# Reordering the first batch's loads and copying block rows of four heads by one DMA, in a block-sparse attention and gated MLP kernel

## The chip, the cores and the metric

The kernel runs on one core of a Trainium2 chip. The core has a matrix engine (TensorE, in the profile PE, with its weight loads as PEld), VectorE (DVE), ScalarE (ACT), GpSimd (POOL) and SyncE (SP), which here only issues DMAs. Sixteen DMA engines move data between device memory and the on-chip memory SBUF. The metric is the device time of one execution in microseconds (us); the time of a kernel is the median of its runs.

## What is computed

The reference is a block-sparse attention (BigBird) followed by a spatial gating MLP (gMLP), cut here to what matters:

```python
# q, k, v: (B=4, H=8, S=768, D=64); blocks of 32 positions, 24 of them
scores = q @ k.T / sqrt(D)
mask = |blk_i - blk_j| <= 1 or blk_i in (0, 23) or blk_j in (0, 23)
mask |= blk_j in sampled_blocks[blk_i]           # 3 drawn blocks per query block
attn = softmax(where(mask, scores, -1e9))
x = (attn @ v) with heads side by side           # (4, 768, 512)

h = relu(x @ w_in)                               # (4, 768, 1024)
u, v = h[..., :512], h[..., 512:]
v_n = (v - mean(v)) / sqrt(var(v) + 1e-6)
v_s = w_spatial @ v_n + b_spatial[:, None]       # over the positions
out = (u * v_s) @ w_out                          # (4, 768, 512)
```

## The kernel before

**Heads and pairs.** The 32 heads of the four batches are taken in 16 pairs p; pairs 0 to 3 are the first batch. For each pair k, q and v are loaded as float32 (tiles `st_k`, `st_q`, `st_v`, made in `load`, L104 to L108), cast to bfloat16 by GpSimd (`cast`, L116 to L135; k and q into a tile `nat`, v into one of six tiles `vv`), and k and q are transposed so that the head dimension lies on the partitions. A load of one pair's k, q or v is 384 KB. Positions are taken in six chunks of 128 (`NCH` = 6), and queries of the first batch in three thirds of two chunks (`NT` = 3, `TC` = 2, `TW` = 256). `C01` are the chunks of the first third, `C03` the first four chunks, `C45` the last two.

**The mask as extra rows of the product.** The tile `kq` has 88 partitions: 64 rows of the transposed k and q and 24 rows (`MR`, one for each block) that carry the mask. Its free dimension is 8 heads times 1536 columns: 768 of k (`K_`) and 768 of q. In the k columns the 24 rows tell the block of each key; in the q columns they hold 0 for an allowed and -300 for a forbidden block. A product over 88 rows gives masked scores at once. These rows are the same for each head. They are made for head 0 (k part by VectorE at L199, the query part by TensorE and a copy, third by third: `mask_rows`, L296; the first two thirds, at L322 and L326, are copied by ScalarE, the last in slot 7) and copied from head 0 to the others by `rows` (L237 to L242), on VectorE in this kernel. `ROWS` (L690) lists those copies as (slot, first head, end head, columns). Pairs of later batches write only the 64 rows of k and q and reuse the mask rows.

**Slots.** The attention runs in slots, one exponential on ScalarE in each. In the first batch, slots 0 to 35, one slot makes scores of 128 x 1024 (`qk_unit`, L389 to L410: four products into one of two PSUM buffers, then the exponential at L410) for a unit of three slots: units 0 and 1 are the heads 0 and 1 with two thirds of the queries, then come pairs 1 to 3 with their first third (slots 6 to 14), pairs 1 to 3 with the second, and all pairs with the last third. The products with v (`av_unit`, L451) follow some four slots behind. From slot 36 on a slot is one chunk of keys of a head (`qk_full`, L418 and L422, and `av_full`, L469). Between them lie the MLP's products (L543), dealt out over the slots from a queue.

**What the change touches.** The order is written out by hand: each engine executes its instructions in the order of the program, and waits for what it needs. `when(slot, ...)` (L684) hangs further work on a slot: `tr_first(p)` (L347) transposes k and the first query third of pair p and copies them into `kq` by VectorE (slots 3, 6, 9 for pairs 1, 2, 3); `tr_rest(p)` (L355) does the other thirds (slots 11, 14, 16, and 17 for pair 0's last); the MLP's first steps, which need the weights `w_in_t`, start in slot 15. The loads of the first batch and of W_in are issued ahead of all slots: at L138 to L149 and, between the casts, at L252 to L275. All but two go by SyncE's queue, and the casts that they feed stand in the same stretch in GpSimd's order.

Of the kernel before, what the change touches and what calls it, by code (L numbers as in the profile page):

```python
# [10 lines left out]
FP32 = mybir.dt.float32  # L11
# [15 lines left out]
def kernel(  # L27
# [16 lines left out]
    nc = tc.nc  # L44

    B, H, S, D = q.shape
    BLK = 32
    NB = S // BLK
    NR = sampled_blocks.shape[1]
    NCH = S // 128  # L50
# [4 lines left out]
    NDM = DM // 128  # L55
# [8 lines left out]
    TC = NCH // NT  # L64
    TW = TC * 128
# [5 lines left out]
    work = ctx.enter_context(tc.tile_pool(name="work", bufs=1))  # L71
# [8 lines left out]
    b_col = const.tile([128, NCH], FP32)  # L80
    mhalf = const.tile([128, NCH], FP32)

    kq = const.tile([KR, H, 2 * S], BF16, name="kq")
    NVV = 6
    vv = [const.tile([128, 2, NCH, VS], BF16, name=f"vv{s}") for s in range(NVV)]
    MR = slice(D, KR)
    K_, Q_ = slice(0, S), slice(S, 2 * S)

    def qcols(t0, n=1):
        return slice(S + t0 * TW, S + (t0 + n) * TW)  # L90


    st = {}

    def dram(src, p, hs=slice(0, 2), cs=slice(0, NCH)):
        b, g = divmod(p, NG)
        return src[b, 2 * g + hs.start:2 * g + hs.stop].rearrange(
            "h (p c) d -> p h (c d)", c=NCH)[:, :, cs.start * D:cs.stop * D]

    H0, H1, BOTH = slice(0, 1), slice(1, 2), slice(0, 2)  # L100
    ALLC, C01, C03, C45 = slice(0, NCH), slice(0, TC), slice(0, 2 * TC), slice(2 * TC, NCH)
    SRC = {"k": k, "q": q, "v": v}

    def load(p, nm, hs=BOTH, cs=ALLC, eng=nc.sync):  # L104
        if (nm, p) not in st:
            st[nm, p] = work.tile([128, 2, S // 2], FP32, tag="st_" + nm, bufs=3, name="st_" + nm)
        eng.dma_start(out=st[nm, p][:, hs, cs.start * D:cs.stop * D],
                      in_=dram(SRC[nm], p, hs, cs))  # L108

# [3 lines left out]
    def nat0_view():  # L113
        return nat[0].rearrange("p c h d -> p (c h d)").rearrange("p (h x) -> p h x", h=2)

    def cast(p, nm, eng, hs=BOTH, cs=ALLC):  # L116
        if nm == "v":
            dst = vv[p % NVV][:, hs, cs, 0:D]
        else:
            if p not in nat:  # L120
                nat[p] = work.tile([128, 2 * NCH, 2, D], BF16, tag="nat", bufs=4, name="nat")
            c0 = 0 if nm == "k" else NCH
            dst = nat[p][:, c0 + cs.start:c0 + cs.stop].rearrange("p c h d -> p h c d")[:, hs]
        src = st[nm, p].rearrange("p h (c d) -> p h c d", d=D)[:, hs, cs]
        if p == 0 and nm != "v":
            dst = nat0_view()[:, hs, (c0 + cs.start) * D:(c0 + cs.stop) * D]
            if cs is not C45:
                dst = dst[:, 0].rearrange("p (i t d) -> p t i d", t=2, d=D)
                src = src[:, 0].rearrange("p (t i) d -> p t i d", t=2)
            else:  # L130
                dst = dst.rearrange("p h (c d) -> p h c d", d=D)
        if eng is nc.scalar:
            nc.scalar.activation(out=dst, in_=src, func=AF.Copy)
        else:
            eng.tensor_copy(out=dst, in_=src)  # L135

    samp = const.tile([KR, 2 * NR], I32)
    load(0, "k", H0, C03, eng=nc.scalar)  # L138
    load(0, "q", H0, C03, eng=nc.scalar)
    nc.sync.dma_start(out=samp[MR], in_=_listify(sampled_blocks).bitcast(I32))  # L140
    load(0, "k", H0, C45)
    load(0, "k", H1)
    load(0, "q", H1, C03)
    load(1, "k")
    load(1, "q")
    load(0, "v")
    load(2, "k")
    load(2, "q")
    load(1, "v")  # L149


    eq = const.tile([KR, NR + 1, NB], FP32)
# [56 lines left out]
    PL, DV = nc.gpsimd, nc.vector  # L209
# [10 lines left out]
    def w_load(key, src):  # L220
        wst[key] = work.tile([128, DM], FP32, tag="osb", bufs=6, name="w_f")
        nc.sync.dma_start(out=wst[key], in_=src)

    def w_in_load(u, g):
        w_load((u, g), moe_w_in[g * 128:(g + 1) * 128, 0 if u else DH:DH if u else DFF])

    def w_in_cast(u, g, eng):
        eng.tensor_copy(out=w_in_t[:, g, 0 if u else DH:DH if u else DFF], in_=wst.pop((u, g)))
# [8 lines left out]
    def rows(hs, cs, eng=nc.vector):  # L237
        src = kq[MR, 0:1, cs].to_broadcast([NB, hs.stop - hs.start, cs.stop - cs.start])
        if eng is nc.scalar:
            nc.scalar.activation(out=kq[MR, hs, cs], in_=src, func=AF.Copy)  # L240
        else:
            eng.tensor_copy(out=kq[MR, hs, cs], in_=src)  # L242
# [7 lines left out]
        nc.gpsimd.memset(vv[s][:, :, :, D:VA], 1.0)  # L250
    nc.gpsimd.memset(mhalf, -0.5)
    cast(1, "k", PL)  # L252
    cast(1, "q", PL)
    cast(0, "v", PL)
    load(3, "k")
    cast(2, "k", PL)
    cast(2, "q", PL)
    cast(1, "v", PL)
    load(3, "q")
    cast(3, "k", PL)  # L260
    cast(3, "q", PL)
    load(2, "v")
    load(0, "q", cs=C45)
    load(3, "v")
    cast(2, "v", PL)
    cast(3, "v", PL)
    cast(0, "q", PL, cs=C45)
    pieces = [(u, g) for u in range(2) for g in range(NDM)]
    for i, x in enumerate(pieces):
        if i >= 6:  # L270
            w_in_cast(*pieces[i - 6], PL)
        w_in_load(*x)
    for x in pieces[2:]:
        w_in_cast(*x, PL)
    nc.sync.dma_start(out=b_col, in_=moe_b_spatial.rearrange("(p c) -> p c", c=NCH))  # L275

# [8 lines left out]
    def bank(nm="ps", tag=None):  # L287
        return psum.tile([128, 1024], BF16, tag=tag or moe_tag(), bufs=2 if tag else 1, name=nm)
# [13 lines left out]
    def head(ps, h, c0, n, at=0):  # L302
        for i in range(0, n, 2):
            nc.tensor.transpose(out=ps[:, at + i * 64:at + (i + 2) * 64],
                                in_=nat0_view()[:, h, (c0 + i) * D:(c0 + i + 2) * D],
                                identity=ident)

    def split0(ps, h, c0, n, t, copy=dve_copy):
        w = n * 64
        copy(kq[0:D, h, c0 * 128 + t * w:c0 * 128 + (t + 1) * w], ps[t * D:(t + 1) * D, 0:w])  # L310
# [14 lines left out]
    split0(psq, 0, *Q4, 1)  # L325
    m1()  # L326

    def second():
        ps2 = bank("ps2", "av")
        head(ps2, 0, *K2)  # L330
        for t in range(2):
            split0(ps2, 0, *K2, t)
        rows(H1, K_)
        rows(H1, qcols(0, 2))
# [349 lines left out]
    def when(slot, *fns):  # L684
        at.setdefault(slot, []).extend(fns)

    def c(f, *a, **kw):
        return lambda: f(*a, **kw)

    ROWS = [(2, 3, 4, K_), (2, 2, 4, qcols(0)), (2, 4, 8, K_), (4, 4, 8, qcols(0, 2)), (13, 2, 4, qcols(1, 2)), (17, 4, 8, qcols(2)),  # L690
            (20, 1, 2, qcols(2))]
    when(0, second)
    when(1, third)
    when(1, c(rows, slice(2, 3), K_))
    when(2, lambda: filler(FILL3, psum.tile([128, 512], FP32, tag=moe_tag(), bufs=1, name="wps")))
    for p, sl in ((1, 3), (2, 6), (3, 9)):
        when(sl, c(tr_first, p))
    for sl, h0, h1, cs in ROWS:
        when(sl, c(rows, slice(h0, h1), cs))
# [64 lines left out]
    def slot_of(p):  # L764
        return S0 + 12 * (p - NG)

    for p in range(NG, NP):
        g = slot_of(p)
# [76 lines left out]
```

## Time and profile before

| what | value |
|---|---|
| runs | 213.68, 212.82, 215.3 us, median 213.68 |
| profiled execution | 212.75 us, its span 210.6 us |
| granted TensorE clock | 0.996 of full speed |
| DMA | 41.82 MB, mean 199 GB/s; 62868 of 63323 packets on the queue of SyncE |
| loads (L107), 384 KB | 4.6 (k), 5.2 (q), 5.7 (v) us median from issue to landing |
| transposes by DMA | 6.7 us (`tt`), 2.8 us (`xt`), 3.1 us (`gt`) median to landing |

The span is what the profile shows of the execution; the metric is about 2 us longer. A row of an order of time reads: start in us, duration in us, engine, line, operation, output<-inputs with partitions x elements, and how many instructions are merged; in brackets the idle time of the engine before it and what ended it. A row of the chain of waits reads: start, duration, engine, output, line. A row of waits reads: who waited, for whom, us in total, times, longest.

### The profile page before, as it was taken

The page shows a single profiled execution, that of the slowest core. Times are in us where ns is not written, and L with a number is a line of the kernel's source. Part 1 is how long each engine was busy: PE and PEld are TensorE (multiplying, and loading weights), DVE is VectorE, ACT ScalarE, POOL GpSimd, SP SyncE. Part 2 cuts the span into 40 slices and gives each one's busy share as a digit, 9 for nine tenths or more (in the row PEclk, how much of TensorE's full clock was granted, in tenths as well). Part 3 has the DMA queues.
Part 4 walks back from the last instruction along what each step waited for, and adds up shares of the span by engine and source line. Part 5 has one row for each costly group of instructions (what it writes and reads, how often), then busy time and mean ns, then how long its engine had stood idle before and what let it go on. Part 6 is the DMA issues. An engine that isn't in the chain of part 4 may idle for free.

```text
span 210.6 us, 5243 instructions
## 1 busy us (share of the span) xinstructions
PE 201.5 (96%) x2113; PEld 128.4 (61%) x2146; DVE 131.7 (63%) x291; ACT 169.2 (80%) x224; POOL 70.0 (33%) x104
## 2 busy tenths in 40 slices
PE   8779999999999999999999999999999999999992
PEld 7569878866566665665655655566555655544441
DVE  7899885979454534384986455286785433576541
ACT  4888999999999999979899788979999787266021
POOL 5696669675663304052341040040120000013000
PEclk9999999999999999999999999999999999999998
DMA  5998799999999999999693597696100324610257
GB/s 151 366 367 315 241 337 278 290 221 292 263 376 200 286 197 306 225 300 313 135 229 64 57 315 166 198 294 138 37 3 19 68 53 91 246 53 2 50 132 266
DMA packets 63323, 41.82 MB, mean 199 GB/s; under 512 B 45124, under 2 KB 58052, under 8 KB 63300
## 3 DMA queue, kind: packets, MB, share of 16 engines
q1 hardware_dynamic: 62868, 41.11, 75.2%
q10 hardware_dynamic: 432, 0.39, 0.6%
q8 instruction: 16, 0.26, 0.5%
q14 instruction: 7, 0.06, 0.1%
HBM read 24.38 MB, written 6.29 MB: 146 GB/s over the span
## 4 chain that ended last, share of the span: by engine, by line
PE 89%; DVE 6%; ACT 2%; issue 2%; ACTq 0%
PE ps_moe L543 31%; PE ps L418 22%; PE ps_av L469 12%; PE ps_t L543 8%; PE ps L405 5%; PE ps_sc L543 4%; PE ps_av L451 3%; DVE kq L242 2%; DVE kq L212 2%; PE wps L180 1%; PE ps L291 1%; ACT a_all L410 1%; ACT osb L215 1%; PE ps_av L291 1%; DVE xn L434 0%
## 5 line engine op out<-in xcount | busy, mean ns | idle before, releaser
L422 ACT ACTIVATE a_all<-ps 128x768 bf16<-128x768 f32 x144 | 113.6, 813 | 14.0 <-PE ps L418 7.3
L418 PE MATMUL ps<-kq 88*128 88x384 bf16 x288 | 70.5, 325 | 0.4
L469 PEld LDWEIGHTS <-a_all 128*128 128x128 bf16 x864 | 45.2, 97 | 19.9
L469 PE MATMUL ps_av<-vv,a_all 128*128 128x65 bf16 x864 | 49.8, 193 | 0.0
L418 PEld LDWEIGHTS <-kq 88*128 88x128 bf16 x288 | 28.0, 98 | 31.1 <-issue 0.9
L543 PE MATMUL ps_moe<-w_in_t,xt 128*128 128x512 bf16 x128 | 39.9, 378 | 0.4
L410 ACT ACTIVATE a_all<-ps 128x1024 bf16<-128x1024 f32 x36 | 35.0, 1024 | 2.4 <-PE ps L405 1.8
L543 PE MATMUL ps_moe<-vn,w_spt 128*128 128x512 bf16 x99 | 30.6, 378 | 0.5
L135 POOL CAST nat<-st_k 128x768 bf16<-128x768 f32 (+2 forms) x17 | 14.8, 875 | 44.4 <-DMA st_k<-in_k_dram 44.3
L433 DVE RECIPROCAL rc<-ps_av 128x6 f32<-128x6 f32 (+1 forms) x36 | 6.7, 185 | 28.8 <-PE ps_av L469 27.9
L611 DVE SCALAR_TENSOR_TENSOR un<-ps_moe,b_col,un 128x512 bf16<-128x512 f32 x18 | 13.5, 749 | 16.3 <-PE ps_moe L543 11.7
L405 PE MATMUL ps<-kq 88*128 88x256 bf16 (+1 forms) x140 | 21.6, 275 | 2.1 <-DVE kq L212 1.5
L580 POOL TENSOR_SCALAR std<-mv 128x3 f32<-128x3 f32 (+1 forms) x9 | 2.1, 238 | 60.7 <-DVE mv L577 44.8
L543 PE MATMUL ps_moe<-w_out_t,gt 128*128 128x512 bf16 x66 | 20.2, 378 | 0.2
L543 PEld LDWEIGHTS <-xt 128*128 128x128 bf16 x192 | 15.5, 98 | 7.2 <-DVE xt L212 0.2
L434 DVE TENSOR_TENSOR xn<-ps_av,rc 128x384 bf16<-128x384 f32 (+1 forms) x36 | 18.5, 513 | 1.2
L576 DVE BATCH_NORM_STATS2 stats<-vn 128x6 f32<-128x512 bf16 x24 | 16.5, 687 | 1.4 <-ACT vn L571 0.9
L405 PEld LDWEIGHTS <-kq 88*128 88x128 bf16 x140 | 12.7, 97 | 5.7 <-DVE kq L212 2.0
L135 POOL CAST vv<-st_v 128x768 bf16<-128x768 f32 x16 | 13.5, 844 | 6.9 <-DMA st_v<-in_v_dram 4.2
L135 POOL CAST nat<-st_q 128x768 bf16<-128x768 f32 (+1 forms) x18 | 13.6, 758 | 5.1 <-DMA st_q<-in_q_dram 4.8
L451 PE MATMUL ps_av<-vv,a_all 128*128 128x65 bf16 x288 | 14.5, 193 | 0.4 <-POOL vv L135 0.4
L451 PEld LDWEIGHTS <-a_all 128*128 128x128 bf16 x288 | 13.5, 97 | 2.0 <-issue 0.6
(79 smaller groups left out, 206.1 us busy)
## 6 DMA issues: line engine op xcount, KB each, us to landing
st_v<-in_v_dram SPq DMA_DIRECT2D x16, 384.0 KB, 5.7
out_dram<-osb SPq DMA_DIRECT2D x23, 256.0 KB, 3.0
st_k<-in_k_dram SPq DMA_DIRECT2D x15, 384.0 KB, 4.6
st_q<-in_q_dram SPq DMA_DIRECT2D x15, 384.0 KB, 5.2
ws_f<-in_moe_w_spatial_dram SPq DMA_DIRECT2D x6, 384.0 KB, 7.5
w_f<-in_moe_w_in_dram SPq DMA_DIRECT2D x8, 256.0 KB, 7.1
w_f<-in_moe_w_out_dram SPq DMA_DIRECT2D x4, 256.0 KB, 4.0
st_q<-in_q_dram SPq DMA_DIRECT2D x2, 128.0 KB, 5.1
```

The source lines that it names most:

```text
L135: eng.tensor_copy(out=dst, in_=src)
L405: nc.tensor.matmul(out=ps[:, at:at + n * TW], lhsT=kq[:, h, ci * 128:(ci + 1) * 128], rhs=kq[:, h, qcols(t0, n)], start=True, stop=True)
L410: nc.scalar.activation(out=out, in_=ps, func=AF.Exp, scale=0.125)
L418: nc.tensor.matmul(out=ps[:, hf * 512:hf * 512 + HALF], lhsT=kq[:, j % H, ci * 128:(ci + 1) * 128], rhs=kq[:, j % H, S + hf * HALF:S + (hf ...
L422: nc.scalar.activation(out=a_ref["h", j][:, ci, :].rearrange("p (b c) -> p b c", b=2), in_=ps.rearrange("p (b c) -> p b c", b=2)[:, :, 0:H ...
L433: nc.vector.reciprocal(out=rc[:, 0:n], in_=ps[:, :, D:VA])
L434: nc.vector.tensor_tensor(out=out, in0=ps[:, :, 0:D], in1=rc[:, 0:n].to_broadcast([128, n, D]), op=ALU.mult)
L451: nc.tensor.matmul(out=av_ref[u][:, to, 0:VA], lhsT=a_ref[u][:, at:at + 128], rhs=vv[pp % NVV][:, h, ci, 0:VA], start=(ci == 0), stop=(ci ...
L469: nc.tensor.matmul(out=av_ref[j][:, qc, 0:VA], lhsT=a_ref["h", j][:, ci, qc * 128:(qc + 1) * 128], rhs=vv[p % NVV][:, h, ci, 0:VA], start= ...
L543: nc.tensor.matmul(out=ref["ps"][:, 0:w], lhsT=lhs(i), rhs=rhs(i), start=(i == 0), stop=(i == n - 1))
L576: nc.vector.bn_stats(out=stats, in_=self.vn[:, tcc, :])
L611: nc.vector.scalar_tensor_tensor(out=self.un[:, tcc, :], in0=ps, scalar=b_col[:, tcc:tcc + 1], in1=self.un[:, tcc, :], op0=ALU.add, op1=AL ...
```

## The change

The tile for q gets four buffers instead of three. Pair 1's query is loaded and cast at first only in its first third. After `k` and the first query third of pair 1 and pair 0's `v`, all further loads and casts of the first batch, and those of W_in, move behind the work on the mask rows of head 0 in the program (L326), in another order, with the query of pairs 1 to 3 in two pieces: the first third (`C01`) and the rest (`C25`). Ahead of them SyncE's queue gets one DMA that copies the 24 mask rows of head 0, the 768 columns of k and the first two query thirds, to heads 4 to 7. The two VectorE copies that did this, in slots 2 and 4, are gone from `ROWS`; those for heads 1 to 3, and those of the last third, stay.

```diff
     ALLC, C01, C03, C45 = slice(0, NCH), slice(0, TC), slice(0, 2 * TC), slice(2 * TC, NCH)
+    C25 = slice(TC, NCH)
...
-            st[nm, p] = work.tile([128, 2, S // 2], FP32, tag="st_" + nm, bufs=3, name="st_" + nm)
+            st[nm, p] = work.tile([128, 2, S // 2], FP32, tag="st_" + nm,
+                                   bufs=4 if nm == "q" else 3, name="st_" + nm)
...
     load(1, "k")
-    load(1, "q")
+    load(1, "q", cs=C01)
     load(0, "v")
-    load(2, "k")
-    load(2, "q")
-    load(1, "v")
...
     cast(1, "k", PL)
-    cast(1, "q", PL)
+    cast(1, "q", PL, cs=C01)
     cast(0, "v", PL)
-    load(3, "k")
-    cast(2, "k", PL)
-    cast(2, "q", PL)
-    cast(1, "v", PL)
-    load(3, "q")
-    cast(3, "k", PL)
-    cast(3, "q", PL)
-    load(2, "v")
-    load(0, "q", cs=C45)
-    load(3, "v")
-    cast(2, "v", PL)
-    cast(3, "v", PL)
-    cast(0, "q", PL, cs=C45)
-    pieces = [(u, g) for u in range(2) for g in range(NDM)]
-    for i, x in enumerate(pieces):
-        if i >= 6:
-            w_in_cast(*pieces[i - 6], PL)
-        w_in_load(*x)
-    for x in pieces[2:]:
-        w_in_cast(*x, PL)
-    nc.sync.dma_start(out=b_col, in_=moe_b_spatial.rearrange("(p c) -> p c", c=NCH))
...
     m1()
+    nc.sync.dma_start(out=kq[MR, 4:H, 0:S + 2 * TW],
+                      in_=kq[MR, 0:1, 0:S + 2 * TW].to_broadcast([NB, H - 4, S + 2 * TW]))
+    load(2, "k")
+    load(2, "q", cs=C01)
+    load(3, "k")
+    load(3, "q", cs=C01)
+    load(1, "v")
+    load(2, "v")
+    load(1, "q", cs=C25)
+    cast(2, "k", PL)
+    cast(2, "q", PL, cs=C01)
+    cast(3, "k", PL)
+    cast(3, "q", PL, cs=C01)
+    cast(1, "v", PL)
+    cast(2, "v", PL)
+    cast(1, "q", PL, cs=C25)
+    w_in_load(0, 0)
+    load(3, "v")
+    w_in_load(0, 1)
+    load(2, "q", cs=C25)
+    w_in_load(0, 2)
+    w_in_load(0, 3)
+    load(3, "q", cs=C25)
+    w_in_load(1, 0)
+    w_in_load(1, 1)
+    load(0, "q", cs=C45)
+    w_in_cast(0, 0, PL)
+    cast(3, "v", PL)
+    w_in_cast(0, 1, PL)
+    cast(2, "q", PL, cs=C25)
+    w_in_cast(0, 2, PL)
+    w_in_cast(0, 3, PL)
+    cast(3, "q", PL, cs=C25)
+    w_in_load(1, 2)
+    w_in_cast(1, 0, PL)
+    w_in_load(1, 3)
+    w_in_cast(1, 1, PL)
+    cast(0, "q", PL, cs=C45)
+    w_in_cast(1, 2, PL)
+    w_in_cast(1, 3, PL)
+    nc.sync.dma_start(out=b_col, in_=moe_b_spatial.rearrange("(p c) -> p c", c=NCH))
...
-    ROWS = [(2, 3, 4, K_), (2, 2, 4, qcols(0)), (2, 4, 8, K_), (4, 4, 8, qcols(0, 2)), (13, 2, 4, qcols(1, 2)), (17, 4, 8, qcols(2)),
+    ROWS = [(2, 3, 4, K_), (2, 2, 4, qcols(0)), (13, 2, 4, qcols(1, 2)), (17, 4, 8, qcols(2)),
             (20, 1, 2, qcols(2))]
```

## The prediction

> **What bounds the kernel now.** I read the page first (shares, slices, chain), then each engine's order of time over the first 25 us, then the waits of SyncE's queue and the traffic by stretches. The page:
>
> ```profile
> span 210.6 us, 5243 instructions
> PE 201.5 (96%) x2113; PEld 128.4 (61%) x2146; DVE 131.7 (63%) x291; ACT 169.2 (80%) x224; POOL 70.0 (33%) x104
> ...
> PE   8779999999999999999999999999999999999992
> ...
> ACT  4888999999999999979899788979999787266021
> ```
>
> Each slice is 5.27 us. PE is full from the fourth slice to the last and ACT is full from the fourth to the fifteenth; what can be gained lies in the first three slices, and it then shifts everything behind. ScalarE's order of time shows how much:
>
> ```profile
> 5.88 5.09 ACT L410 ACTIVATE a_all<-ps 128x1024 bf16<-128x1024 f32 x5 [0.36 <-PE ps L405]
> 11.22 1.02 ACT L410 ACTIVATE a_all<-ps 128x1024 bf16<-128x1024 f32 x1 [0.25 <-PE ps L405]
> 12.72 3.07 ACT L410 ACTIVATE a_all<-ps 128x1024 bf16<-128x1024 f32 x3 [0.48 <-PE ps L405]
> 16.11 1.02 ACT L410 ACTIVATE a_all<-ps 128x1024 bf16<-128x1024 f32 x1 [0.32 <-PE ps L405]
> 17.41 22.48 ACT L410 ACTIVATE a_all<-ps 128x1024 bf16<-128x1024 f32 x23 [0.28 <-PE ps L405]
> ```
>
> One exponential is one slot of the schedule. After slot 0 starts at 5.88 four gaps come, ahead of slots 5, 6, 9 and 10: 0.25 + 0.48 + 0.32 + 0.28 = 1.33 us. Behind 17.41 there is none for 23 slots. The chain of waits in that stretch says what PE lacked, and the orders of time of VectorE and GpSimd (cut to single instructions) say why:
>
> ```profile
> 8.43 2.88 DVE kq L242 x4
> 11.33 0.68 DVE kq L212
> 12.05 0.69 DVE kq L212
> 12.77 1.30 DVE kq L242
> ```
>
> ```profile
> 8.43 0.91 DVE L242 COPY kq<-kq 24x768 bf16<-24x768 bf16 x1
> 9.26 0.34 DVE L242 COPY kq<-kq 24x768 bf16<-24x768 bf16 x1
> 10.36 0.94 DVE L242 COPY kq<-kq 24x3072 bf16<-24x3072 bf16 x1
> ...
> 12.77 1.30 DVE L242 COPY kq<-kq 24x2048 bf16<-24x2048 bf16 x1
> ```
>
> ```profile
> 8.30 0.83 POOL L135 CAST nat<-st_q 128x768 bf16<-128x768 f32 x1 [0.26 <-DMA st_q<-in_q_dram]
> 9.31 0.98 POOL L135 CAST vv<-st_v 128x768 bf16<-128x768 f32 x1 [0.18 <-DMA st_v<-in_v_dram]
> 10.37 1.62 POOL L135 CAST nat<-st_k 128x768 bf16<-128x768 f32 x1
> 11.94 0.82 POOL L135 CAST nat<-st_q 128x768 bf16<-128x768 f32 x1
> ```
>
> Slot 5 waits for v0's cast (PE stands 0.43 us until 10.29). Slot 6 waits for pair 1's copies at 11.33, which stand behind the block rows. Slots 9 and 10 follow pair 2, whose q cast ends at 12.76 and whose copies stand behind the 1.30 us row copy. The same 24x768 copy takes 0.91 us beside a running cast and 0.34 without one, and the k cast beside the 24x3072 copy takes 1.62 instead of 0.82: the two engines hold each other up.
>
> **The change, part by part.** *Row copies.* The 24x3072 and 24x2048 copies leave VectorE: 0.94 + 1.30 = 2.24 us, all in the chain. The copies for heads 2 and 3 stay: the first at 8.43 (q1's cast is now over), 0.35; the second at worst behind v0's cast, which ends near 9.4, then 0.34; the 24x512 0.28. Pair 1's first copy starts near 10.05 instead of 11.33 and lasts 0.68; before, that copy's end at 12.01 was followed by its exponential at 12.72, 0.71 later, so now it could run at 11.45. ScalarE has slot 5 until 5.88 + 6 x 1.02 = 12.0. That gap goes.
>
> *Order of loads.* From 6 to 19 us the 16 DMA engines moved 374 GB/s at a busy share of 1.06, so order is what counts: 384 KB cost 1.05 us, 256 KB 0.70, 128 KB 0.35. Start from v0's landing before, 9.27 (issue at 3.56 plus 5.7). Two thirds of q1 no longer go ahead of it: 9.27 - 0.70 = 8.57, its cast 8.6 to 9.4, and slot 5's 0.25 us goes too. (Now PE had to wait till 10.29.)
>
> *The broadcast DMA.* 24 rows x 4 heads x 1280 x 2 B = 0.246 MB. Nothing in the trace copies rows within SBUF without transposing. Bounds: 0.66 us of the engines at the loads' 374 GB/s; 2.0 us at the 124 GB/s of 34 to 36 us, when they were mostly transposing. I take 1.0, near the loads, because its runs are 2560 B long like theirs are 1536, but only 24 rows take part. The Trainium skill, "DMA: Bandwidth & Descriptors", section "Why a DMA increments its semaphore by 16 and not by 1", says a transfer uses the largest number of engines up to 16 that divides its slowest dimension, here 12 of 16; "SBUF — State Buffer", section "Door 1: The DMA port swizzle", would let rows 64 to 87 reach 6 of 16 ports at 27.2 GB/s, an estimate of 1.5 us, and the sum below would be 0.5 us worse. No row here shows either. SyncE holds this DMA until ScalarE's second mask-row copy has ended (4.83 + 0.70 = 5.53), and k2 and all loads behind it wait in the queue: k2 goes out near 6.1 rather than 4.08. What covers this is the backlog: k0 to v0 are 1.57 MB, which last until about 7.5, and a load needs some 1.5 us from issue to moving (first issue 0.72, traffic from 2.2). Without that cover: up to 0.5 us, inside my upper bound of 2.0. PE needs these rows at slot 9, about 14; the DMA lands near 9.6.
>
> *Pair 2.* Landing: k2 9.57 + 1.05 = 10.62, its first query third 10.97; casts of 0.82 and 0.40 end at 11.84 (before: 12.76). Pair 2's transposes and the next scores took 1.05 us (12.77 to 13.82), so slot 7's exponential could start at 12.89; it is due at 5.88 + 7 x 1.02 = 13.02. Free by 0.13. VectorE then has pair 2's copies (1.40) done near 14, and slot 9 is due at 15.06. The gaps of 0.32 and 0.28 go.
>
> *Late loads.* Going on: k3 12.02, q3 third 12.37, v1 13.42, v2 14.47, q1 rest 15.17, W_in 15.87, v3 16.92, W_in 17.62, q2 rest 18.32, W_in 19.02 and 19.72, q3 rest 20.42, W_in 21.12 and 21.82, q0 rest 22.17. SP's own pace does not limit this: the waits of its queue show an issue held until the load eight issues earlier has landed, and eight loads are some 5 us of traffic.
>
> ```profile
> SPq L222 <- DMA st_v<-in_v_dram: 2.4, 2, 2.0
> ```
>
> GpSimd's work is the same but for splitting three query casts (0.40 + 0.62 for 0.82, 0.6 us in all). PE reached the transposes of the query rests at 18.14, 21.10, 22.90 and 24.25 for pairs 1, 2, 3 and 0; 1.33 earlier that is 16.81, 19.77, 21.57, 22.92. The casts end at 15.8, 18.9, 21.0 and 22.8 by the landings above: in time, the last by 0.1. But before, the landings trailed this rule from 15 us on: v2 16.9 for 15.57, v3 18.35 for 17.0. With that 1.3 us W_in ahead of it is also late, q0's cast ends near 24.1, 1.2 us after PE wants it, and PE, full there, loses that. I cannot say whether the trail comes back; half of it, 0.65 us, costs 0.65 - 0.1 = 0.55. The old kernel hid these casts (q0's rest at 19.16, wanted 24.25); this one spends that slack.
>
> *Nothing else:* the fourth q buffer takes away a wait of SP (issues at 6.26, then 9.16) and no instruction; loads for pair 4 can go at about 19.5 instead of 22.48, and nobody on the chain waits for them.
>
> Sum: -1.33 + 0.55 = -0.8 us. The profiled execution took 212.75 (span 210.6), so 211.95 in its terms. The runs before gave 212.75, 212.82, 213.68 and 215.3, median 213.25 of the four; 213.25 - 0.8 = 212.45, say **212.4**. The likeliest case's own range, from no trail to the whole one, is a gain of 1.33 to 0.1: 211.9 to 213.1.
>
> **Rivals.** *Slower: the queue comes late.* Let b be the broadcast's engine time and t the trail. q0's rest is late by (b - 1.0) + t - 0.1 (the margin above), with PE blocked in order ahead of the next scores; pair 2's casts cost b - 1.13 by themselves. The gain is gone when b + t exceeds 2.4. At b = 2.0 and t = 1.3 the loss is 2.2 us, net +0.9: 214.15 on the median's scale. At b = 3.3 and no less t it is +2.2, 215.5. For it: the trail is in the trace. Against it: the transposes, the only rows for a large b, are another kind of transfer.
>
> *No change: something else takes the gaps.* The 24x512 copy could fall behind k2's cast (10.62 to 11.44): pair 1's copy then starts 11.45, and slot 6 runs at 12.85, as late as before. Or PE, without idle from 16 us on, keeps its pace and the start is absorbed. Either leaves 213.25, perhaps 0.2 around. Against: VectorE has about 0.6 us before k2 lands, and PE's order follows ScalarE slot by slot.
>
> *Full gain and a little more:* no trail, and the 0.15 us gap at 40.04 goes as well: -1.5, 211.75.
>
> *It does not do what it says*, the rows still waited for on slot 9: that needs the DMA to land after 14, 4 us late, and is the first rival's extreme.
>
> **How the numbers follow.** Chances: forecast 0.5, full gain 0.14, no change 0.18, slower 0.18. Low end: the full gain less 0.9 for the scatter of runs (the four lie 2.5 us apart), 210.8. High end: the slower rival's first price with 0.5 us of scatter, 214.7. About 1% (2.1 us) is what a measurement can tell from no change. No case reaches -2.1 by itself; with that scatter I give 0.2 for faster by more, three in ten of the gaining cases' 0.64. Slower by more needs b near 3.3 or scatter on the slower rival: 0.14. Within 1%: 0.66.
>
> **What would show it.** Right: ScalarE without gaps from 5.88 to slot 17; v0's cast starting near 8.6; pair 2's q cast ending near 11.8; no 24x3072 copy; slot 10 near 16.1 instead of 17.41. The broadcast's issue to landing near 3.6 us (6.0 to 9.6) is right for b = 1.0. Wrong: PE waiting for the casts L135 at pair 2's transposes (a large b) or at the transposes of q3's or q0's rest near 22 to 24 (the trail); ScalarE's gaps moved to slots 12 to 18; or a start 1.3 us earlier that is gone by 43 us, where the full-width slots begin.

## The result and the profile after

The changed kernel takes 215.7 us (median of 13 runs, 214.74 to 217.96) against 213.87 for the kernel before (13 runs, 212.6 to 216.63); the ratio is 1.0111, 95% interval 1.0085 to 1.0138. Some executions of either kernel ran longer at a lower granted clock; the ratios and intervals here leave these out and the medians do not, so a ratio need not be the quotient of two medians. The changed kernel is about 1.1% slower. The forecast of 212.4 and its range up to 214.7 were wrong, and so was the direction. The profiled execution took 215.24 us, 2.49 more than before.

The page of the changed kernel, busy times and slices:

```profile
span 213.5 us, 5247 instructions
...
PE 201.7 (94%) x2111; PEld 128.3 (60%) x2146; DVE 131.2 (61%) x289; ACT 169.0 (79%) x224; POOL 70.2 (33%) x107
...
PE   7789899999999999989999999999999999999991
...
ACT  3978899999999999969999788979999786275021
```

The engines do the same work as before (PE 201.7 for 201.5, ACT 169.0 for 169.2), so 2.9 us of span are waits. PE lost a tenth in its first, fifth, eighteenth and last slice and gained one in its third; of the first five slices ScalarE gained one in its second and lost one in its first, third and fifth. Four marks show where the time went (start of each, in us; the output products are the last ones of the last batch, and the last column is the start of their last group of four):

| | first exponential | slot 36 | last batch's first product | first output product | last group of output products |
|---|---|---|---|---|---|
| before | 5.88 | 42.81 | 182.97 | 201.43 | 206.27 |
| after | 6.11 | 43.97 | 184.65 | 203.12 | 208.97 |
| lost in the stretch | 0.23 | 0.93 | 0.52 | 0.01 | 1.01 |

So 1.16 us are lost by slot 36, where I forecast a start 1.33 us earlier or one whose gain a late cast gives back; 0.52 near 90 us; 1.01 behind the first output product, a place the prediction does not mention. ScalarE's order of time after (start, duration, in brackets the idle time before it):

```profile
6.11 4.83 ACT L430 ACTIVATE a_all<-ps 128x1024 bf16<-128x1024 f32 x5 [0.42 <-PE ps L425]
11.09 1.94 ACT L430 ACTIVATE a_all<-ps 128x1024 bf16<-128x1024 f32 x2 [0.16 <-PE ps L425]
13.99 2.86 ACT L430 ACTIVATE a_all<-ps 128x1024 bf16<-128x1024 f32 x3 [0.96 <-PE ps L425]
17.17 1.94 ACT L430 ACTIVATE a_all<-ps 128x1024 bf16<-128x1024 f32 x2 [0.32 <-PE ps L425]
19.40 2.85 ACT L430 ACTIVATE a_all<-ps 128x1024 bf16<-128x1024 f32 x3 [0.29 <-PE ps L425]
22.65 1.94 ACT L430 ACTIVATE a_all<-ps 128x1024 bf16<-128x1024 f32 x2 [0.40 <-PE ps L425]
24.89 1.02 ACT L430 ACTIVATE a_all<-ps 128x1024 bf16<-128x1024 f32 x1 [0.30 <-PE ps L425]
26.23 14.82 ACT L430 ACTIVATE a_all<-ps 128x1024 bf16<-128x1024 f32 x15 [0.31 <-PE ps L425]
```

The 0.48 ahead of slot 6 is gone, as planned, and slot 5's 0.25 is 0.16. In their place stands 0.96 ahead of slot 7, and gaps of 0.3 to 0.4 go on to 26 us. What PE waited for between 4 and 43 us (total, times, longest), GpSimd's order of time, and SyncE's queue:

```profile
PE ps L269 <- POOL nat L137: 1.7, 3, 0.9
```

```profile
9.34 0.83 POOL L137 CAST vv<-st_v 128x768 bf16<-128x768 f32 x1 [1.09 <-DMA st_v<-in_v_dram]
12.00 0.83 POOL L137 CAST nat<-st_k 128x768 bf16<-128x768 f32 x1 [1.84 <-DMA st_k<-in_k_dram]
12.77 0.40 POOL L137 CAST nat<-st_q 128x256 bf16<-128x256 f32 x1
...
24.95 0.40 POOL L137 CAST nat<-st_q 128x256 bf16<-128x256 f32 x1
```

```profile
5.71 0.97 SPq L306 DMA_DIRECT2D kq<-kq  x1
6.72 0.53 SPq L109 DMA_DIRECT2D st_k<-in_k_dram  x1
7.30 1.20 SPq L109 DMA_DIRECT2D st_q<-in_q_dram  x1
8.60 0.41 SPq L109 DMA_DIRECT2D st_k<-in_k_dram  x1
```

The three waits are at the transposes of pair 2 (0.9) and of the query rests of pairs 1 and 2 (0.41 each): all for casts, and these (GpSimd idle 1.84 us ahead of k2's) for loads. k2's cast starts at 12.00, where its load was forecast to have landed at 10.62; that of q0's last third starts at 24.95, where it was forecast to be over at 22.8. The broadcast waited for the mask rows until 5.70, its issue took SyncE another 0.97 us, and k2 went out at 6.72 (before: 4.08; forecast: near 6.1). The traffic from 7 to 12 us goes with it (columns: stretch, its length, busy us and count of PE, PEld, DVE, ACT and POOL, granted clock, DMA share, GB/s), before and then after:

```profile
7.00:12.00 5.00, 3.52 (x40) 2.29 (x39) 4.83 (x10) 4.57 (x5) 4.26 (x5) 1.00 1.06 376
```

```profile
7.00:12.00 5.00, 4.08 (x52) 2.96 (x51) 3.71 (x11) 4.81 (x6) 2.08 (x3) 1.00 0.96 230
```

The DMA engines count as busy for 0.96 of the stretch and move 230 GB/s for 376: their packets take longer. In the trace the broadcast is 96 packets of 2560 B, from 7.32 to 9.82 us. Their median is 231 ns, where a load's packet of 1536 B takes 65.

At the end, PE's order of time; the bracket is a wait for the last transpose of the gated product by DMA, which the kernel before does not have (there the same two groups start at 205.84 and 206.27 without a wait):

```profile
205.77 1.89 PE L563 MATMUL ps_t<-w_out_t,gt 128*128 128x512 bf16 x8
208.52 0.61 PE L563 MATMUL ps_sc<-w_out_t,gt 128*128 128x256 bf16 x4 [0.87 <-DMA gt<-un]
208.97 0.60 PE L563 MATMUL ps_t<-w_out_t,gt 128*128 128x256 bf16 x4
```

### The profile page after: what moved, and what is told of

Same layout as the page of the kernel before. It is cut to its first block, busy times and chain, and to the rows that moved or that the text cites. A ratio compares the mean times of both kernels' runs of the same rounds, so it can differ in the third digit from the quotient of the medians.

```text
span 213.5 us, 5247 instructions
## 1 busy us (share of the span) xinstructions
PE 201.7 (94%) x2111; PEld 128.3 (60%) x2146; DVE 131.2 (61%) x289; ACT 169.0 (79%) x224; POOL 70.2 (33%) x107
## 4 chain that ended last, share of the span: by engine, by line
PE 79%; DMA 9%; ACT 2%; DVE 2%; issue 2%; SPq 2%; POOL 1%; ACTq 0%; DVEq 0%
PE ps_moe L563 30%; PE ps L438 22%; PE ps_av L489 12%; PE ps_t L563 5%; PE ps L425 4%; DMA st_v<-in_v_dram 3%; DMA st_k<-in_k_dram 2%; PE ps_sc L563 2%; PE ps_av L471 2%; DMA gt<-un 2%; DMA st_q<-in_q_dram 1%; ACT a_all L430 1%; SPq L641 1%; DVE kq L211 1%; PE ps L269 1%
## 5 line engine op out<-in xcount | busy, mean ns | idle before, releaser
L489 PEld LDWEIGHTS <-a_all 128*128 128x128 bf16 x864 | 45.2, 97 | 20.0
L563 PE MATMUL ps_moe<-vn,w_spt 128*128 128x512 bf16 x97 | 30.1, 378 | 0.4
L137 POOL CAST nat<-st_k 128x768 bf16<-128x768 f32 (+2 forms) x17 | 13.7, 808 | 46.0 <-DMA st_k<-in_k_dram 44.8
L631 DVE SCALAR_TENSOR_TENSOR un<-ps_moe,b_col,un 128x512 bf16<-128x512 f32 x18 | 13.5, 749 | 16.1 <-PE ps_moe L563 13.9
L137 POOL CAST nat<-st_q 128x768 bf16<-128x768 f32 (+2 forms) x21 | 14.8, 703 | 5.0 <-DMA st_q<-in_q_dram 4.7
L211 DVE COPY kq<-tt 64x1536 bf16<-64x1536 bf16 x24 | 15.9, 661 | 0.3
```

Source lines behind the costliest of these rows:

```text
L211: nc.vector.tensor_copy(out=o, in_=i)
L489: nc.tensor.matmul(out=av_ref[j][:, qc, 0:VA], lhsT=a_ref["h", j][:, ci, qc * 128:(qc + 1) * 128], rhs=vv[p % NVV][:, h, ci, 0:VA], start= ...
L563: nc.tensor.matmul(out=ref["ps"][:, 0:w], lhsT=lhs(i), rhs=rhs(i), start=(i == 0), stop=(i == n - 1))
L631: nc.vector.scalar_tensor_tensor(out=self.un[:, tcc, :], in0=ps, scalar=b_col[:, tcc:tcc + 1], in1=self.un[:, tcc, :], op0=ALU.add, op1=AL ...
```

## The experiments

Three theories stood against each other for the start: that of the broadcast (D: it holds SyncE's queue and slows the loads behind it), that of the order of loads (O: the split queries come too late whoever copies the rows), and, for the copies on VectorE, that one of them can be put later without any DMA. A fourth, F, came up for the tail (the stretch from the first to the last group of output products): PE's program has grown by a few instructions, and a packet of its code now moves at a bad moment. BC stands for the two lines of the broadcast (L306, L307). All medians are beside the runs of the kernel before on the same chip, 213.5 to 213.8. There are 12 runs each of e1, e2, e4 and e9 to e12, 10 of e7 and e8, 6 of e3 and 4 of e6.

In their first 22 us six of the profiles hold a stretch in which the granted TensorE clock was 0.50, beside waits of PE of 1.0 to 2.8 us: e3 from 11.05 to 17.88, e4 from 18.44 to 21.85, e5 from 13.20 to 16.61, e6 from 16.30 to 19.71, e10 from 11.17 to 17.99 and e12 from 12.82 to 16.23. The two kernels' first profiles have none there, nor have e7, e8 and e11, where PE had waits of 1.3 to 1.4 us; what brings it on is not shown. An asterisk marks the six, and their slot 36 is not read as an effect of the edit. The others need care too: e2 and e11 differ by two idle products ("fillers") at the start and are 1.03 us apart at slot 36. One mark is therefore read across all traces: with the new order of loads, k2's cast starts at 11.80 to 12.51 in the four with the broadcast as it is or in two parts (the change, e4, e7, e10), and at 9.81 to 10.27 in the five without (e1, e2, e8, e11, e12).

| kernel | median, us | ratio to before (95%) | slot 36 at | tail, first to last output product |
|---|---|---|---|---|
| e1_order_only | 212.91 | 0.997 (0.9931 to 1.001) | 41.96 | 5.58 |
| e2_rows_late | 212.97 | 0.9985 (0.9948 to 1.0022) | 41.53 | 5.54 |
| e3_broadcast_only | 217.3 | 1.0166 (1.0117 to 1.0214) | 46.18* | 5.61 |
| e4_change_again | 215.61 | 1.0088 (1.0051 to 1.0126) | 46.61* | 5.82 |
| e5_before_again (one run) | 215.93 | – | 45.71* | 4.76 |
| e6_second_copy | 216.65 | 1.0106 (1.0028 to 1.0183) | 45.94* | 5.56 |
| e7_rows_16_and_8 | 215.23 | 1.0059 (1.0022 to 1.0095) | 44.40 | 5.56 |
| e8_hold_only | 213.95 | 1.0037 (0.9994 to 1.0079) | 42.95 | 5.52 |
| e9_before_two_fillers_more | 213.62 | 1.0007 (0.9978 to 1.0037) | 43.56 | 5.55 |
| e10_change_two_fillers_less | 215.34 | 1.0065 (1.003 to 1.0099) | 45.82* | 4.75 |
| e11_rows_late_two_fillers_less | 212.59 | 0.9968 (0.9929 to 1.0008) | 42.56 | 4.84 |
| e12_order_only_two_fillers_less | 212.7 | 0.996 (0.9921 to 0.9999) | 44.55* | 4.82 |

**e1: the order alone, the rows back on VectorE in their old slots.**

```diff
-    BC
...
-    ROWS = [(2, 3, 4, K_), (2, 2, 4, qcols(0)), (13, 2, 4, qcols(1, 2)), (17, 4, 8, qcols(2)),
+    ROWS = [(2, 3, 4, K_), (2, 2, 4, qcols(0)), (2, 4, 8, K_), (4, 4, 8, qcols(0, 2)), (13, 2, 4, qcols(1, 2)), (17, 4, 8, qcols(2)),
```

> The change without its DMA: new order of loads and casts, four q buffers, and the two copies of heads 4 to 7 back on VectorE in slots 2 and 4. Theory D (the broadcast DMA itself is what costs: half-rate traffic from 7.4 to 9.9 us and SyncE held ahead of it): with it gone k2's cast starts near 9.8 instead of 12.0, PE's waits of 0.9 and 0.4 us at the transposes of pairs 1 to 3 shrink to under 0.3 in all, ratio to before 0.994 to 1.000. Theory O (the order: query rests come too late, whatever the DMA does): PE still waits 0.4 us and more at the rests of pairs 1 and 2, ScalarE still has gaps ahead of slots 12, 15, 17 and 18, ratio 1.003 to 1.010.

**e2: as e1, but the 24x3072 copy in slot 3, behind pair 1's copies.**

```diff
-    BC
...
-    ROWS = [(2, 3, 4, K_), (2, 2, 4, qcols(0)), (13, 2, 4, qcols(1, 2)), (17, 4, 8, qcols(2)),
+    ROWS = [(2, 3, 4, K_), (2, 2, 4, qcols(0)), (3, 4, 8, K_), (4, 4, 8, qcols(0, 2)), (13, 2, 4, qcols(1, 2)), (17, 4, 8, qcols(2)),
```

> As the run without the DMA, but the 24x3072 copy of the mask rows stands in slot 3 behind pair 1's copies on VectorE instead of slot 2 ahead of them, in time that VectorE idled in the changed kernel (10.9 to 12.0 us). Theory D: all four early gaps of the kernel before go (1.33 us) and none comes, ratio 0.992 to 0.997, faster than both kernels. Theory O: 1.000 to 1.008.

Without the DMA, PE waits for no query rest, and both reach slot 36 earlier than the kernel before: by 0.85 us in e1 and by 1.28 in e2. So the order of loads is not what costs. The whole times agree: the intervals of e1 and e2 end at 1.001 and 1.0022, that of e4, the change run beside them, begins at 1.0051. ScalarE in e2:

```profile
6.11 4.83 ACT L428 ACTIVATE a_all<-ps 128x1024 bf16<-128x1024 f32 x5 [0.44 <-PE ps L423]
11.08 4.75 ACT L428 ACTIVATE a_all<-ps 128x1024 bf16<-128x1024 f32 x5 [0.15 <-PE ps L423]
16.06 25.57 ACT L428 ACTIVATE a_all<-ps 128x1024 bf16<-128x1024 f32 x26 [0.23 <-PE ps L423]
```

Slot 10 is at 16.06; the prediction named 16.1 as the sign of success. In this trace the gaps are closed by the order of loads and a copy put one slot later, without the DMA (in e11, below, one of them is back). In the whole time little is left of it (212.9 and 213.0, both intervals hold 1; for e2 less had been expected, 0.997 at most): the tail takes 0.7 us back, 5.5 for 4.84.

**e3: the broadcast alone, with the loads in their old order behind it and whole queries.**

```diff
-                                    bufs=4 if nm == "q" else 3, name="st_" + nm)
+            st[nm, p] = work.tile([128, 2, S // 2], FP32, tag="st_" + nm, bufs=3, name="st_" + nm)
...
-    load(1, "q", cs=C01)
+    load(1, "q")
...
     BC
     load(2, "k")
-    load(2, "q", cs=C01)
-    load(3, "k")
-    load(3, "q", cs=C01)
+    load(2, "q")
     load(1, "v")
-    load(2, "v")
-    load(1, "q", cs=C25)
+    load(3, "k")
...
```

> The broadcast DMA at its place and the two VectorE copies gone, but whole queries, three q buffers, and behind the DMA the loads and casts in the order of the kernel before. Theory D: at least as slow as the change, since q1's other two thirds (0.7 us of traffic) now also stand ahead of k2: k2's cast starts at 12.3 to 13, PE waits over 1 us at pair 2's transposes, ratio 1.008 to 1.020. Theory O: the rests are in time again, so no waits but the one at pair 2, ratio 0.997 to 1.004.

The worst of all, 1.0166. GpSimd's casts of v0 and k2, each waiting for its load:

```profile
11.48 0.83 POOL L136 CAST vv<-st_v 128x768 bf16<-128x768 f32 x1 [1.21 <-DMA st_v<-in_v_dram]
13.07 0.83 POOL L136 CAST nat<-st_k 128x768 bf16<-128x768 f32 x1 [0.76 <-DMA st_k<-in_k_dram]
```

v0, at 9.31 in the kernel before, comes 2.2 us later, and PE waits 1.3 us for it and 1.2 for k2. v0 was issued ahead of the broadcast; that the broadcast slows the loads already under way fits this, but is not shown, because in e5, the kernel before without any broadcast, v0's cast also starts as late as 10.85. Nor is it known how much of the 1.0166 these waits make: all six runs have a mean granted clock of 0.978 to 0.984, and in this trace it was 0.50 for 6.8 us.

**e4 and e5: the change and the kernel before, unaltered.**

> The changed kernel unaltered, for a second profile. Ratio 1.009 to 1.014. In the first profile the start cost 1.2 us by slot 36 and another 1.4 to 1.7 us came behind it (0.5 us at an output copy, 0.9 us at the last transpose). If that second part belongs to the change, this profile has it at the same two places; if it is the scatter of one execution, it does not.

> The kernel before, for a second profile. In its first profile PE waited nowhere behind 43 us; every other kernel so far had PE wait 0.6 to 0.9 us for the last transpose, and three of them 0.2 to 0.5 us at an output copy near 90 us. If those waits belong to the new kernels, this profile has none of them; if the first profile was a lucky one, it has at least the first, and its span is 211.2 or more.

e4 gives the loss a second time: 1.0088, and the wait for the last transpose too, 0.86 us. e5 is a single run, whose 215.93 lies among the longer ones of that kernel; its tail is as short as in the first profile of that kernel, 4.76 us and no wait for a transpose. Its start is not: v0's load landed at 10.79 instead of 9.26, PE waited 1.0 us for its cast, and with the stretch at half clock slot 36 came 2.9 us later than in the first profile. So 1.16 us at slot 36 between two executions prove nothing alone; the repeated casts and the whole times do.

**e6: a second broadcast right behind the first, of 4 x 1152 columns, into a tile that is written anew later (an extra copy that nobody reads).**

```diff
+    nc.sync.dma_start(out=w_spt[MR].rearrange("p a b c -> p (a b c)").rearrange("p (h n) -> p h n", h=4),
+                      in_=kq[MR, 0:1, 0:1152].to_broadcast([NB, 4, 1152]))
```

> The change with a second broadcast DMA right behind the first, of the same shape but 1152 instead of 1280 columns, into memory that is not in use yet. Theory D (the broadcast moves at some 100 GB/s and everything behind it waits): k2's cast starts 2.2 to 3.0 us later than in the change (14.2 to 15.0), ratio 1.020 to 1.026. If it is only the wait of SyncE's queue for the mask rows that costs, the second copy adds no more than 0.7 us, ratio 1.012 to 1.015.

```profile
14.02 0.83 POOL L137 CAST nat<-st_k 128x768 bf16<-128x768 f32 x1 [3.22 <-DMA st_k<-in_k_dram]
```

k2's cast moves from 12.00 to 14.02, 2.0 us for 0.9 of the bytes, so such a copy costs the loads behind it 2 us or a little more. PE pays it at pair 2: it waits 2.3 us at the transposes for 0.9, and slot 7 moves from 13.99 to 16.02, ahead of the stretch at half clock. In the 2.0 us that slot 36 comes later (45.94 for 43.97) this wait and the half clock can't be told apart. The ratio, 1.0106 where 1.020 to 1.026 had been expected, is no higher than the change's; with four runs its interval is too wide to show the 2 us or to rule them out.

**e7: the broadcast in two DMAs, of 16 and of 8 rows.**

```diff
-    BC
+    for r0, r1 in ((D, D + 16), (D + 16, KR)):
+        nc.sync.dma_start(out=kq[r0:r1, 4:H, 0:S + 2 * TW],
+                          in_=kq[r0:r1, 0:1, 0:S + 2 * TW].to_broadcast([r1 - r0, H - 4, S + 2 * TW]))
```

> The broadcast in two DMAs, rows 64 to 79 and rows 80 to 87, all else as in the change. If the number of engines (12) sets its pace, the larger part goes over 16 and the 2560 B packets keep their 231 ns; the whole is then no slower than the change, k2's cast at 11.5 to 12.2, ratio 1.007 to 1.012. If the rows set it (few rows share one way into SBUF), the first part's packets take 350 ns or more, and k2's cast starts later than 12.2, ratio 1.010 to 1.018.

From 7.15 to 9.83 us, k2's cast at 11.96 instead of 12.00: nothing gained there. The 64 packets of the 16 rows have a median of 392 ns, those of the 8 rows, which come last, 102 ns. Each theory has one of its signs: the packets those of the rows, k2's cast those of the engines. Splitting the rows changed the packet's time and not the sum. That fits a limit in the rows' way into or out of SBUF rather than in the number of DMA engines; it is the reading I take, it is not shown, and no run separates the two ways.

**e8: e2, with SyncE held as the broadcast holds it, but by a copy of 24 rows by 16 columns into an unused tile.**

```diff
-    BC
+    scrap = const.tile([KR, 1, 16], BF16, name="scrap")
+    nc.sync.dma_start(out=scrap[MR], in_=kq[MR, 0:1, S + 2 * TW - 16:S + 2 * TW])
```

> The version with the rows late on VectorE and no broadcast, but SyncE's queue held as in the change: ahead of k2 it issues a copy of 16 columns of the 24 mask rows (0.8 KB) that has to wait for the same ScalarE copy. It tells the hold from the traffic. Theory D: k2 goes out at 6.0 to 6.7, its cast starts at 10.0 to 10.6 instead of 10.0 to 10.3, and the ratio stays at 0.995 to 1.001. If the hold is what costs, k2's cast starts at 11.5 or later and the ratio is 1.005 or more.

The traffic from 7 to 12 us in e2 and in e8, and two of e8's casts:

```profile
7.00:12.00 5.00, 4.10 (x56) 3.11 (x56) 4.77 (x13) 4.82 (x6) 3.90 (x5) 1.00 1.04 350
```

```profile
7.00:12.00 5.00, 4.49 (x61) 3.49 (x61) 4.77 (x11) 4.96 (x6) 3.38 (x5) 1.00 0.87 274
```

```profile
9.81 0.83 POOL L137 CAST nat<-st_k 128x768 bf16<-128x768 f32 x1
...
17.43 0.62 POOL L227 CAST w_in_t<-w_f 128x512 bf16<-128x512 f32 x1 [1.41 <-DMA w_f<-in_moe_w_in_dram]
```

The hold alone leaves the engines short of work: (350 - 274) GB/s x 5 us = 0.38 MB, 1.0 us at the 371 GB/s of the stretch behind it. k2 itself isn't late (9.81), but the loads behind it are: GpSimd stands 1.11 us for k3, whose cast then starts at 12.10 as in e2 (12.11), and the first W_in cast is at 17.43 for 15.80. In the change the same stretch lost (350 - 230) x 5 = 0.60 MB and carried 0.246 MB of the broadcast: 0.85 MB of loads, 2.3 us, of which by this estimate 1.0 is the hold and the other 1.3 the copy's own packets. In the whole time the hold gives 1.0037, between e2's 0.9985 and the change's 1.0111; its interval overlaps e2's and e4's, so the split rests on one trace of each. (Of slot 36's 1.42 us against e2, 0.82 is there by slot 10, behind a gap of 1.10 ahead of slot 9; e2 does not have this gap, and e11 has it without a hold.)

**e9 to e12: two fillers (four TensorE instructions) more in the kernel before, two less in the change, in e2 and in e1.**

```diff
-    FILL, FILL2, FILL3 = 26, (4, 0, 3), 4
+    FILL, FILL2, FILL3 = 28, (4, 0, 3), 4      # e9; 24 in e10, e11 and e12
```

> The kernel before with 28 instead of 26 idle products on zeros at the start, four more TensorE instructions. Theory F (code loading): in the changed kernel and all seven variants TensorE has one to three more semaphore instructions, and the 17th 16 KB packet of its code's queue moves at 203 to 208 us, among the last transposes, and not after the end as in both profiles of the kernel before; PE then waits 0.5 to 0.9 us for the last transpose. With four more instructions the kernel before must show the same: the packet 1 to 4 us ahead of the last output product, PE's wait, 5.5 to 5.9 us from the first to the last output product of the last batch instead of 4.8, ratio 1.001 to 1.006. If it is something else, 4.8 us stays and the ratio is 0.998 to 1.002.

> The change with 24 instead of 26 idle products at the start, so that TensorE's code is shorter than before's by one instruction. Theory F: the 17th packet goes behind the end, no wait for the last transpose, 4.8 us at the tail, ratio 1.004 to 1.008 instead of 1.009 to 1.011; what is left is the start's. Else: 1.009 to 1.012.

> The version without the broadcast and with the rows late on VectorE, with 24 idle products. By both theories the version that beats both kernels: slot 36 about 1.2 us earlier than before and the tail as short as before's, ratio 0.990 to 0.996.

> The change without its DMA, rows on VectorE in slots 2 and 4, with 24 idle products: slot 36 about 0.8 us earlier than before and the short tail, ratio 0.992 to 0.997.

PE's end of e9, and then of e11:

```profile
204.74 1.89 PE L543 MATMUL ps_t<-w_out_t,gt 128*128 128x512 bf16 x8
207.22 0.61 PE L543 MATMUL ps_sc<-w_out_t,gt 128*128 128x256 bf16 x4 [0.59 <-DMA gt<-un]
```

```profile
204.34 1.89 PE L561 MATMUL ps_t<-w_out_t,gt 128*128 128x512 bf16 x8
206.07 0.60 PE L561 MATMUL ps_sc<-w_out_t,gt 128*128 128x256 bf16 x4
```

Two fillers more put the wait into a kernel that had none; two fewer take it out of one that had it. The trace has a queue named "instruction" with 17 packets of 16 KB (about 1 us each, one every 6 to 13 us in most of the kernel) in every kernel; I take it for TensorE's code, since four TensorE instructions move it. The wait goes with the start of the last one:

```text
kernel           last code packet, us   wait for the transpose, us
before           211.7                  none
before again     215.2                  none
e10, e11, e12    211.8, 211.2, 213.8    none
after, e4        206.5, 208.9           0.87, 0.86
e1, e2           203.5, 203.5           0.65, 0.61
e3, e6, e7, e8   207.9 to 204.5         0.53 to 0.68
e9               205.1                  0.59
```

Theory F stands for the tail in every kernel: among the last DMA transposes the packet costs 0.5 to 0.9 us of waiting, behind them nothing. The last transpose itself landed 3.9 to 4.3 us after its issue where the packet ran among them, and 2.4 to 2.5 where it did not (in the ten traces that record the landing). Before, PE's stream has 6 semaphore instructions; with the change 9, and 7 or 8 in e1, e3 and e8: the other order asks for other synchronization, and that is enough. The whole time shows less: each of e10, e11 and e12 is lower than its pair (1.0065 for 1.0111, 0.9968 for 0.9985, 0.996 for 0.997), e9 is 1.0007, and every one of these steps is within the intervals. The ratios of e9 and e11 lie outside what theory F had been expected to give (1.001 to 1.006 and 0.990 to 0.996). e12 has the lowest ratio, 0.996 with an interval just under 1; its profiled execution, with 214.44 us well above its median, has a gap of 1.41 us ahead of slot 6. One step is clear: e10 and e11 both have the short tail and differ only in how heads 4 to 7 get their rows, and their intervals, 1.003 to 1.0099 and 0.9929 to 1.0008, do not meet. So the broadcast costs about 1% of the whole time, the tail apart.

**What the copies on VectorE bring with them.** e8 and e11 show gaps of 1.10 and 1.13 us ahead of slot 9 and e12 one of 1.41 ahead of slot 6; e2 has none at either, only 0.23 ahead of slot 10. In all three PE waits for VectorE's copies (1.3 to 1.5 us), which stand behind the row copies. In e11 these run beside GpSimd's casts:

```profile
11.49 0.95 DVE L241 COPY kq<-kq 24x3072 bf16<-24x3072 bf16 x1
12.37 1.30 DVE L241 COPY kq<-kq 24x2048 bf16<-24x2048 bf16 x1
```

The two copies take 0.95 and 1.30 us, and k3's cast beside them 1.54 for 0.82. The same instructions meet in e11 and largely miss each other in e2, which differs by two fillers, so the start gains 1.3 us in one trace and less in another.

## Why the prediction was wrong, point by point

**Row copies: right.** Both copies are gone from the chain, pair 1's first copy starts at 9.50 (I had 10.05), and slot 6's gap is gone.

**Order of loads: right in part.** e2's slot 10 at 16.06 and 1.28 us by slot 36 are the forecast's 16.1 and 1.33, with some luck, since e11 with the same order gains 0.25. In the change v0's cast came at 9.34 instead of 8.6. The broadcast is not the cause that can be shown: e2, without it, has 9.18, the others of the same order without it 8.71 to 8.98, and e7, with it, 8.51. Why v0 comes late in some executions stays open.

**The broadcast DMA: the step that failed, in its size.** "I take 1.0, near the loads, because its runs are 2560 B long like theirs are 1536, but only 24 rows take part" took the wrong neighbour: a packet of it took 231 ns, 3.6 times a load's for 1.7 times the bytes. And "what covers this is the backlog" was wrong about the hold: the cover holds for k2, as e8 shows, but the engines run short of work behind it, 1.0 us of traffic; "up to 0.5 us, inside my upper bound" was half of it. Both together put q0's rest at 24.95 against e2's 22.22: b is 2.7, above the bound of 2.0 I had given it. Against e1, e12 and e11, where that cast starts at 22.80, 22.57 and 23.48, b is 2.2, 2.4 and 1.5: more than the 1.0 taken in each, above the bound in three of four. That bound, from the transposes' 124 GB/s, gives 2.0 us for the copy alone; the copy took 2.5 (0.246 MB from 7.32 to 9.82, 98 GB/s with the loads beside it).

From the Trainium skill, "SBUF — State Buffer", section "Door 1: The DMA port swizzle", came the estimate of 1.5 us for these rows; it points the right way, and with it the sum would have been 0.5 us worse, but the trace has 2.5. By the rule of the Trainium skill, "DMA: Bandwidth & Descriptors", section "Why a DMA increments its semaphore by 16 and not by 1", 16 rows would go over 16 engines and 24 rows over 12; in e7 the 16 rows went no faster than the 24 in the change (0.164 MB in 1.9 us, 87 GB/s, for 98).

**Pair 2: wrong for that reason.** Its margin was 0.13 us; k2's cast came 1.38 later than k2's forecast landing, PE waited 0.91 at the transposes, and slot 7 lost 0.96.

**Late loads: mechanism right, place wrong.** In e2 there is no broadcast, and q0's rest was cast at 22.22, by the rule without b due 1.0 us earlier (22.17 - 1.0 = 21.17): the trail t is near 1.0, where I took 0.65 from a range of 0 to 1.3. It cost e2 nothing. In e1, e11 and e12 t is 1.4 to 2.3, so how 24.95 - 21.17 = 3.8 us divides into b and t changes from execution to execution. The sum is beyond the 2.4 from which the rival decides, and its formula gives -1.33 + 3.8 - 1.0 - 0.1 = +1.4 us; slot 36 is 1.16 later. So the rival *the queue comes late* describes the start in its mechanism: loads late behind the broadcast. The place differs: PE lost the time at pair 2 and at the rests of pairs 1 and 2, and came to q0's rest late enough, so that the two figures agree is partly luck.

**"Nothing else": wrong.** The tail's 1.01 us has no term in the sum. I counted the instructions that do work and not where the code of PE ends. With it, the change comes to 1.16 + 0.52 + 1.01 = 2.7 us at the last output product, and 2.9 in the span. That the rival's extreme of 215.5 is near the 215.7 measured is partly chance, since a third of the loss comes from here. And 0.6 of the 3.3 us between 212.4 and 215.7 is the base: four runs of the kernel before had a median of 213.25, thirteen have 213.87.

**The 0.52 us near 90 us** is a wait of PE for a VectorE copy of an output, behind another that takes 1.11 us beside a GpSimd cast instead of 0.54. The second profile of the kernel before (e5) has such a wait as well (0.55), and e6, with the broadcast, has none; I count it as scatter. No run was made to show that the change never causes it.

The chances were wrong with the size: 0.18 for a mechanism that needed b + t above 2.4, when nothing in the trace showed a copy within SBUF and the upper bound was one row of another kind of transfer.

## What to carry over

A DMA that is free of the engines isn't free of the queue: price what its wait and its issue keep from going out (here 1.0 us of load traffic), and what a transfer on few rows does to the packets beside it (231 ns for 2560 B). Where loads feed the bound, first try the other order and a later slot for the copy; here that gave up to 1.3 us at the start, and a whole time no slower than before. And look at the end of a kernel after an edit at its beginning, as the place where a packet of code falls can move by a few instructions.

## What was not expected of the hardware

- Copying 24 rows within SBUF by DMA, loads beside it, ran at 98 GB/s (0.246 MB in 2.5 us), where loads from device memory ran at 371 to 376. The median of its packets of 2560 B was 231 ns (192 to 224 in e3, e4, e6 and e10); in e7 it was 392 ns for the first 16 rows and 102 ns for the last 8.
- Issuing the broadcast kept SyncE for 0.97 us, and the load after the next for 1.20; most issues of loads took 0.37 to 0.55, but one in the kernel before took 0.96.
- What I take for TensorE's code came in packets of 16 KB, 0.9 to 1.8 us each and one of 2.5. Four TensorE instructions more or fewer moved the last one by 5 to 10 us and with it a wait of 0.5 to 0.9 us.
- In six of fourteen profiles the granted TensorE clock was 0.50 for 3.4 or 6.8 us within the first 22 us, in e5 also for the kernel before.
